# Turning two heads' out^T in one 128-row transpose, in an attention and feed-forward kernel

## Chip, cores and metric

The kernel runs on one core of a Trainium2 chip. The metric is the time of one execution on the device in microseconds; lower is better. Five engines work side by side, each through its own instructions in order: TensorE (PE in the profile; its weight loads PEld), VectorE (DVE), ScalarE (ACT), GpSimd (POOL) and SyncE (SP), whose queue issues the DMAs here.

## What is computed

Attention over 2 batches x 8 heads, 1152 keys of 64 dimensions, with neighbouring queries averaged in pairs (576 queries), then two gated feed-forward layers over the 1152 tokens. All is float32.

```python
q_pool = q.reshape(B, H, S // 2, 2, D).mean(axis=3)          # B, H, S, D = 2, 8, 1152, 64
scores = scale * np.matmul(q_pool, k.transpose(0, 1, 3, 2))
attn = np.exp(scores - scores.max(-1)); attn = attn / (attn.sum(-1) + 1e-09)
x = (attn @ v) -> (B * S // 2, H * D)                          # 1152 tokens of 512
xn = x / sqrt(mean(x * x) + 1e-06) * rms_g                     # layer 1
x = (silu(xn @ w_gate) * (xn @ w_val)) @ w_out                 # d_ff 1536
out = (sigmoid(x @ w_gate2) * (x @ w_val2)) @ w_out2           # layer 2
```

## The kernel before

**Tiles and chunks.** The 576 queries of a head are five chunks: chunks 1 to 4 hold 128 queries each, and chunk 0, the odd one, the last 64. Part 0 of a head is chunks 0 to 2 (320 queries), part 1 chunks 3 and 4 (256). Heads go in pairs (0 and 1, 2 and 3, ...); a pair's Q and K are loaded and turned together, the two heads side by side in 128 columns. Head 0 of a pair is called the even one here, head 1 the odd one.

**The stages of attention.** Scores (`s_unit`): PE multiplies Q by 384 keys at a time into a PSUM bank `s`, DVE (L543) copies the bank to `e` and takes the maximum, ACT exponentiates. For each head there are then 18 units, one for each key block of 128 and each part. A unit (`t_unit`) turns its two or three blocks of `e` by PE transposes into a bank `eT`; ACT, DVE or POOL copies the bank out, as high and low parts (`et`) or as one float32 (`ef`). Some slots later `av_unit` multiplies by V and adds up in a bank `o`: 128 columns for `et`, two products of 64 columns side by side for `ef`. A bank `o` has two halves of 64 partitions whose sum is out^T. After the last key block ACT copies one half to `osb` and DVE adds the other. The banks rotate: two for `s`, four for `eT` and all other transposes, two for `o`.

**Where the change works.** `o_step` turns out^T back: for each chunk of a part PE takes `osb` (64 partitions x 128 queries) as a transpose of 64 rows into the bank `oT`; ACT copies `oT` to `os` (L650), POOL multiplies by the reciprocal of the sums, `rcp`, into `x` (L648). So a head has two groups of oT, one of three and one of two transposes. In before the odd chunk is cut short elsewhere too: Q's sum of neighbours has a POOL instruction of its own for chunk 0 with 64 rows (L353), `q_transposes` turns chunk 0 with 64 rows through the helper `transpose` (L380), and so does `tr` in `x_steps` for the odd chunk of x, four transposes of 64 rows in each batch. `load_pair` fills only rows 0 to 63 of chunk 0 of Q.

**Order.** The order is written by hand: `at(g, rank, fn)` puts a step into slot g, and `run_agenda` writes the slots out in order, by rank within a slot. A head takes 18 slots. Every engine then goes through its own instructions in that order, and waits where a tile is not ready or a bank is still read. The scores of a pair are put 15 slots ahead of its use. At the end of attention the slots are filled with the first feed-forward products, while x of batch 1 is normed and turned. In the layers each weight block is loaded and split into two parts (L244 to L285) while earlier ones are in use.

Of the kernel before, what the change touches and what calls it, by code (L numbers as in the profile page):

```python
# [16 lines left out]
P = 128  # L17
# [78 lines left out]
def tile_attention_moe_moe(ctx, tc, q, k, v, w_gate1, w_val1, w_out1, rms_g, w_gate2, w_val2, w_out2, out):  # L96
# [234 lines left out]
    def load_pair(p):  # L331
        b, hp = divmod(p, NPAIR)
        kr = ap.tile([P, NK, P], F32, tag="kraw", bufs=1, name="kraw")
        qr = ap.tile([P, 2, NQC, 2 * D], F32, tag="qraw", bufs=1, name="qraw")
        qs = q[b, 2 * hp:2 * hp + 2].rearrange("j (s two) d -> j s (two d)", two=2)
        for j in range(2):
            nc.sync.dma_start(qr[:, j, 1:NQC, :], qs[j, 0:SQ - QH, :].rearrange("(c p) e -> p c e", p=P))
        nc.sync.dma_start(qr[0:QH, :, 0, :], qs[:, SQ - QH:SQ, :].rearrange("j p e -> p j e"))
        for j in range(2):

            nc.sync.dma_start(kr[:, :, j * D:(j + 1) * D], k[b, 2 * hp + j].rearrange("(p c) d -> p c d", c=NK))
        raw[p] = (kr, qr)
# [5 lines left out]
    def pool_q(p):  # L348
        kr, qr = raw[p]
        qs = ap.tile([P, NQC, P], F32, tag="qsum", bufs=1, name="qsum")  # L350
        qd = qs.rearrange("p c (j d) -> p j c d", j=2)
        nc.gpsimd.tensor_tensor(qd[:, :, 1:NQC], qr[:, :, 1:NQC, 0:D], qr[:, :, 1:NQC, D:2 * D], op=ALU.add)
        nc.gpsimd.tensor_tensor(qd[0:QH, :, 0], qr[0:QH, :, 0, 0:D], qr[0:QH, :, 0, D:2 * D], op=ALU.add)  # L353
        raw[p] = (kr, qs)

    def prep_v(i):
# [9 lines left out]
            nc.tensor.transpose(t[:, c * P:(c + 1) * P], raw[p][0][:, 4 * g + c, :], ident)  # L366
        return t[:, 0:n * P], slice(4 * g * P, (4 * g + n) * P)

    def q_transposes(p, g):
        t = bank("t", "qT")  # L370
        c0, c1 = ((0, 3), (3, NQC))[g]
        cs = slice(QCOL[c0], QCOL[c1] if c1 < NQC else SQ)
        for c in range(c0, c1):
            transpose(t, QCOL[c] - cs.start, raw[p][1][:, c, :], c)
        return t[:, 0:cs.stop - cs.start], cs

    def transpose(t, o, x, c, half=0):

        r = slice(0, P) if c else slice(half * QH, (half + 1) * QH)
        nc.tensor.transpose(t[:, o:o + r.stop - r.start], x[r], ident[r, r])  # L380
# [13 lines left out]
    def prep_first():  # L394
# [47 lines left out]
            return t[HP, 0:3 * P], slice(3 * g * P, 3 * (g + 1) * P)  # L442

        def head0(g0, is_k, g):
            t, cs = k_group(0, g) if is_k else q_transposes(0, g)
            if is_k:
                at(g0, 12, lambda: nc.scalar.activation(ka[HP, cs], t, AF.Copy))
                at(g0, 16, lambda: nc.vector.tensor_tensor(ka[LP, cs], t, ka[HP, cs].bitcast(F32), op=ALU.subtract))
            else:
                at(g0, 12, lambda: nc.scalar.activation(qa[:, 0, cs], t, AF.Copy, scale=QSC))  # L450
                at(g0, 16, lambda: nc.vector.scalar_tensor_tensor(qa[:, 1, cs], t, QSC, qa[:, 0, cs].bitcast(F32), op0=ALU.mult, op1=ALU.subtract))

        def head1(g0, is_k, g):
            t, cs = k_group(1, g) if is_k else q_transposes(0, g)
            hi, lo = (kb[HP, cs], kb[LP, cs]) if is_k else (qb[:, 0, cs], qb[:, 1, cs])
            sc = 1.0 if is_k else QSC
            at(g0, 13, lambda: nc.scalar.activation(hi, t, AF.Copy, scale=sc))
            if (is_k, g) in SECOND_DVE:
                at(g0 + 1, 19, lambda: nc.vector.scalar_tensor_tensor(lo, t, sc, hi.bitcast(F32), op0=ALU.mult, op1=ALU.subtract))
                return  # L460
            r = ae.tile([P, 512], F32, tag="kqt", bufs=3, name="kqt")[0:t.shape[0], 0:t.shape[1]]
            at(g0, 13, lambda: nc.scalar.activation(r, t, AF.Copy, scale=sc))
            at(g0 + 1, 21, lambda: nc.gpsimd.tensor_tensor(lo, r, hi.bitcast(F32), op=ALU.subtract))
# [44 lines left out]
    def s_unit(g, p, k):  # L508
# [40 lines left out]
                nc.gpsimd.tensor_copy(sums[i + 1][h * QH:(h + 1) * QH, 0:1], sums[i][(1 - h) * QH:(2 - h) * QH, 0:1])  # L549

        def recip():
            rcp[i] = ae.tile([P, NQC, 1], F32, tag="rc", bufs=2, name="rc")
            nc.vector.tensor_scalar_add(sums[i], sums[i], 1e-9)
            nc.vector.reciprocal(rcp[i][:, :, 0], sums[i])

        at(g, 17, top)
        if u == NSU - 1:
# [46 lines left out]
    def av_unit(g, i, j, et, parts):  # L604
        part, kc = part_of(i, j)
        n = NB if part else NA
        if kc == 0:
            oacc[i, part] = bank("o", "o")
        o = oacc[i, part]
        if parts:  # L610
            for k in range(2):
                nc.tensor.matmul(o[:, 0:n], vv[i][:, kc, :], et[:, k, 0:n], start=(kc == 0 and k == 0), stop=(kc == NK - 1 and k == 1))  # L612
        elif kc % 2 == 0:
            ets[i] = et
        else:

            for r, c, x in ((HP, kc - 1, ets[i]), (LP, kc, et)):
                nc.tensor.matmul(o[r, 0:n], vraw[i][:, c, :], x[:, 0:n], start=(kc == 1), stop=False)  # L618
        if kc == NK - 1:
            if i not in osb:  # L620
                osb[i] = ae.tile([D, SQ], F32, tag="osb", bufs=2, name="osb")
            ob = osb[i][:, part * NA:part * NA + n]
            at(g, 11, lambda: nc.scalar.activation(ob, o[HP, 0:n], AF.Copy))
            at(g, 18, lambda: nc.vector.tensor_tensor(ob, o[LP, 0:n], ob, op=ALU.add))
            g += 1 if i == NHEAD - 1 and part else 2
            at(g, 7, lambda: o_step(g, i, part))

    def o_step(g, i, part):

        b, h = divmod(i, H)  # L630
        if b not in xall:
            if b == B - 1:
                xa = ae.tile([P, NCA, DM], F32, tag="xa", bufs=1, name="xa")
                xb = ae.tile([P, NQC - NCA, DM], F32, tag="xb", bufs=1, name="xb")
            else:

                xa, xb = [xpool.tile([P, NDM * (NT - NX0) // DM, DM], F32, tag=f"x{s}1", name="x") for s in "hl"]
            xall[b] = ((xa, 0, NCA), (xb, NCA, NQC))
        x, c0, c1 = xall[b][part]
        n = c1 - c0  # L640
        t = bank("t", "oT")
        for c in range(c0, c1):
            nc.tensor.transpose(t[:, (c - c0) * D:(c - c0 + 1) * D], osb[i][:, QCOL[c]:QCOL[c] + P], ident[HP, HP])  # L643
        os = ae.tile([P, NCA, D], F32, tag="os", bufs=1, name="os")[:, 0:n]
        xs = x[:, 0:n, h * D:(h + 1) * D]

        def norm():
            nc.gpsimd.tensor_tensor(xs, os, rcp[i][:, c0:c1, :].to_broadcast([P, n, D]), op=ALU.mult)  # L648

        at(g + 1, 14, lambda: nc.scalar.activation(os.rearrange("p c d -> p (c d)"), t[:, 0:n * D], AF.Copy))  # L650
        at(g + 1, 41, norm)
        if h == H - 1:
            x_steps(g + 2, b, part)

    def x_steps(g, b, part):
# [28 lines left out]
        def tr(g, c):  # L684
            t = bank("o" if last else "t", "xT")
            for dc in range(NDM):
                transpose(t, dc * P, xp[:, c, dc * P:(dc + 1) * P], c0 + c)
            n = P if c0 + c else QH
            src = t.rearrange("p (c f) -> p c f", f=P)
            t0 = b * SQ + ((c0 + c - 1) * P if c0 + c else SQ - QH)  # L690
# [240 lines left out]
```

## Time and profile before

| | |
|---|---|
| median of three runs | 763.41 us (762.86 to 763.51) |
| the profiled execution | 763.09 us, span 761.3 us |
| PE busy | 751.4 us, 99% of the span |
| DVE, ACT, POOL busy | 464.8, 420.4, 391.1 us |
| opening, attention, hand-over, layers | about 0 to 31, to 292, to 320, to the end |
| oT transposes | 80, of 64 rows |

The profile names a line L..., an engine, an operation and the tiles written and read (out<-in). Matmuls on PE overlap: each is listed with its whole length, and the next one starts before it ends. What one costs is therefore seen in the starts of its neighbours. In a timeline consecutive instructions of one line and tile are merged, with their count (x3). A transpose is a matmul with the tile as its weights and an identity as the moving data, and the form 64*128 means 64 rows and 128 columns of the array; 128*64 is 128 rows and 64 columns.

### The profile page before, as it was taken

The page shows a single profiled execution, that of the slowest core. Times are in us where ns is not written, and L with a number is a line of the kernel's source. Part 1 is how long each engine was busy: PE and PEld are TensorE (multiplying, and loading weights), DVE is VectorE, ACT ScalarE, POOL GpSimd, SP SyncE. Part 2 cuts the span into 40 slices and gives each one's busy share as a digit, 9 for nine tenths or more (in the row PEclk, how much of TensorE's full clock was granted, in tenths as well). Part 3 has the DMA queues.
Part 4 walks back from the last instruction along what each step waited for, and adds up shares of the span by engine and source line. Part 5 has one row for each costly group of instructions (what it writes and reads, how often), then busy time and mean ns, then how long its engine had stood idle before and what let it go on. Part 6 is the DMA issues. An engine that isn't in the chain of part 4 may idle for free.

```text
span 761.3 us, 13230 instructions
## 1 busy us (share of the span) xinstructions
PE 751.4 (99%) x4865; PEld 696.0 (91%) x4865; DVE 464.8 (61%) x1150; ACT 420.4 (55%) x903; POOL 391.1 (51%) x456
## 2 busy tenths in 40 slices
PE   8999999999999999999899999999999999999998
PEld 6678888889888888999799999999999999999998
DVE  7777787878787887766666675442265546453000
ACT  6577777778887875454544444533354445445100
POOL 6567678678787771244443445743254345437100
PEclk9999999999999999999999999999999999999999
DMA  8535463827274210033322232431122222222101
GB/s 224 113 76 125 121 150 84 185 50 183 67 165 100 70 44 1 29 96 98 93 79 82 81 111 87 136 111 56 56 83 84 84 84 85 82 84 84 63 1 63
DMA packets 70400, 69.82 MB, mean 92 GB/s; under 512 B 19200, under 2 KB 61824, under 8 KB 70336
## 3 DMA queue, kind: packets, MB, share of 16 engines
q1 hardware_dynamic: 70336, 68.99, 33.1%
q8 instruction: 38, 0.62, 0.3%
q14 instruction: 26, 0.21, 0.1%
HBM read 52.17 MB, written 2.36 MB: 72 GB/s over the span
## 4 chain that ended last, share of the span: by engine, by line
PE 94%; DVE 2%; ACT 1%; issue 1%; POOL 1%; DMA 0%; ACTq 0%
PE acc L760 38%; PE s L539 11%; PE acc L878 10%; PE acc L855 10%; PE eT L380 9%; PE o L612 7%; PE o L618 4%; PE eT L579 2%; PE oT L643 1%; DVE e L543 1%; PE kT L366 1%; PE qT L380 1%; PE xT L380 1%; DMA first<-in_q_dram 0%; ACT wg L244 0%
## 5 line engine op out<-in xcount | busy, mean ns | idle before, releaser
L760 PE MATMUL acc<-xh,w 128*128 128x384 f32 (+2 forms) x1184 | 298.5, 333 | 3.1 <-DVE sg L773 3.0
L760 PEld LDWEIGHTS acc<-xh,w 128*128 128x128 f32 x1184 | 212.6, 188 | 4.7 <-DVE sg L773 4.6
L760 PE MATMUL acc<-xl,w 128*128 128x384 f32 (+2 forms) x592 | 196.4, 332 | 0.0
L285 POOL TENSOR_TENSOR w<-wr,w 128x512 fp32r<-128x512 f32 x72 | 101.8, 1414 | 154.4 <-ACT w L284 154.4
L543 DVE TENSOR_SCALAR_CACHE_REDUCE e<-s 128x384 f32<-128x384 f32 (+1 forms) x219 | 120.3, 554 | 46.7 <-PE s L539 43.3
L244 ACT ACTIVATE wg<-wraw 128x512 f32<-128x512 f32 x72 | 48.3, 670 | 150.4 <-issue 111.2
L272 POOL TENSOR_TENSOR wr<-wsg,wr 128x512 uint32<-128x512 uint32 x72 | 93.3, 1296 | 65.3 <-DVE wsg L271 62.2
L380 PE MATMUL eT<-ident,e 128*128 128x128 f32 (+1 forms) x594 | 113.8, 275 | 0.0
L539 PE MATMUL s<-kk,qq 128*128 128x384 f32 (+1 forms) x396 | 110.0, 362 | 1.4 <-DVE e L543 1.1
L760 PEld LDWEIGHTS acc<-xl,w 128*128 128x128 f32 x592 | 111.1, 188 | 0.0
L558 ACT ACTIVATE e<-e,nb 128x1152 f32<-128x1152 f32 (+1 forms) x73 | 91.4, 1252 | 0.3 <-DVE nb L545 0.3
L380 PEld LDWEIGHTS eT<-ident,e 128*128 128x128 f32 (+1 forms) x594 | 76.4, 140 | 16.3 <-issue 6.0
L612 PE MATMUL o<-et,vv 128*128 128x320 f32 (+1 forms) x380 | 90.4, 334 | 0.0
L774 DVE TENSOR_TENSOR sg<-acc,sg 128x384 f32<-128x384 f32 (+2 forms) x74 | 40.5, 547 | 75.4 <-PE acc L760 40.4
L878 PE MATMUL acc<-w,hh 128*128 128x256 f32 x432 | 76.7, 281 | 0.0
L599 ACT ACTIVATE et<-eT 128x320 fp32r<-128x320 f32 (+1 forms) x139 | 56.4, 414 | 34.5 <-PE eT L380 28.7
L539 PEld LDWEIGHTS s<-kk,qq 128*128 128x128 f32 (+1 forms) x396 | 61.2, 187 | 15.2 <-DVE e L543 4.8
L855 PE MATMUL acc<-hh,w 128*128 128x384 f32 x288 | 73.5, 335 | 0.0
L271 DVE SCALAR_TENSOR_TENSOR wsg<-wg,wsg 128x512 uint32<-128x512 uint32 x72 | 65.5, 910 | 2.3
L878 PEld LDWEIGHTS acc<-w,hh 128*128 128x128 f32 x432 | 66.5, 189 | 0.0
L781 DVE TENSOR_TENSOR hl<-sg,hh 128x384 fp32r<-128x384 f32 (+2 forms) x74 | 62.9, 851 | 4.0 <-ACT hh L780 4.0
L600 DVE TENSOR_TENSOR et<-eT,et 128x320 fp32r<-128x320 f32 (+1 forms) x139 | 63.3, 457 | 3.1 <-ACT et L599 2.4
(113 smaller groups left out, 1132.3 us busy)
## 6 DMA issues: line engine op xcount, KB each, us to landing
wraw<-in_moe_w_gate_dram SPq DMA_DIRECT2D x24, 512.0 KB, 3.6
wraw<-in_moe_w_val_dram SPq DMA_DIRECT2D x24, 512.0 KB, 3.6
wraw<-in_moe_w_out_dram SPq DMA_DIRECT2D x24, 512.0 KB, 3.7
qq<-qq SPq DMA_DIRECT2D x21, 288.0 KB, 3.2
vraw<-in_v_dram SPq DMA_DIRECT2D x16, 288.0 KB, 2.9
kraw<-in_k_dram SPq DMA_DIRECT2D x14, 288.0 KB, 5.5
kk<-kh SPq DMA_DIRECT2D x14, 288.0 KB, 4.1
kk<-kl SPq DMA_DIRECT2D x14, 288.0 KB, 4.7
```

Of the source, the lines that this page charges most:

```text
L271: nc.vector.scalar_tensor_tensor(sg, g, 3, sg, op0=ALU.logical_shift_left, op1=ALU.bitwise_or)
L272: nc.gpsimd.tensor_tensor(r, sg, r, op=ALU.add)
L285: nc.gpsimd.tensor_tensor(t[:, 1], r, t[:, 0].bitcast(F32), op=ALU.subtract)
L380: nc.tensor.transpose(t[:, o:o + r.stop - r.start], x[r], ident[r, r])
L539: nc.tensor.matmul(s[r, 0:SU], qs, ks[:, kc], start=(n1 == 0), stop=(n1 == len(products) - 1))
L543: nc.vector.tensor_scalar(e[r, kc], s[r, 0:SU], 1.0, None, op0=ALU.mult, op1=ALU.max, accum_out=m[r, u:u + 1])
L558: at(g + EXP_LAG, 12, lambda: nc.scalar.activation(e[r], e[r], AF.Exp, bias=nb[r], scale=1.0, accum_out=sums[i][r, c:c + 1]))
L600: at(g + 1, 20, lambda: nc.vector.tensor_tensor(et[:, 1, 0:n], t, et[:, 0, 0:n].bitcast(F32), op=ALU.subtract))
L612: nc.tensor.matmul(o[:, 0:n], vv[i][:, kc, :], et[:, k, 0:n], start=(kc == 0 and k == 0), stop=(kc == NK - 1 and k == 1))
L760: nc.tensor.matmul(acc[:, 0:nt], wt[:, ws, dc * P:(dc + 1) * P], xs[:, dc], start=(dc == 0 and n == 0), stop=(dc == NDM - 1 and n == 2))
L855: nc.tensor.matmul(acc[t][:, 0:NTT], w[:, ws, (fc % 4) * P:(fc % 4 + 1) * P], hs[fc][:, cs], start=(fc == 0 and n == 0), stop=(fc == NFC - ...
L878: nc.tensor.matmul(acc[r // 2][:, (r % 2) * HC:(r % 2 + 1) * HC], hs[fc][:, r * P:(r + 1) * P], w[:, ws, (fc % 2) * HC:(fc % 2 + 1) * HC], ...
```

## The change

Both heads of a pair put their out^T into one `osb` of 128 partitions: the even head into partitions 0 to 63, the odd one into 64 to 127 (ACT and DVE swap the halves of `o` for it). `o_step` is only called behind the odd head, and turns both heads at once, with 128 rows and the whole identity. The reciprocals of both heads lie in one tile `rcp` with two columns per chunk, `os` and POOL's product are twice as wide. For the odd chunk of Q rows 64 to 127 are filled with queries that nobody uses (one more DMA per pair, of the first 64 queries), POOL's sum is one instruction, and the transpose has 128 rows; its 64 superfluous columns are written over by the next chunk's transpose. Pair 0, whose Q is loaded in another way, keeps its 64 rows. The odd chunk of x is turned with 128 rows too.

```diff
@@ -335,7 +335,9 @@
         qs = q[b, 2 * hp:2 * hp + 2].rearrange("j (s two) d -> j s (two d)", two=2)
         for j in range(2):
             nc.sync.dma_start(qr[:, j, 1:NQC, :], qs[j, 0:SQ - QH, :].rearrange("(c p) e -> p c e", p=P))
-        nc.sync.dma_start(qr[0:QH, :, 0, :], qs[:, SQ - QH:SQ, :].rearrange("j p e -> p j e"))
+
+        for r, x in ((slice(0, QH), SQ - QH), (slice(QH, P), 0)):
+            nc.sync.dma_start(qr[r, :, 0, :], qs[:, x:x + QH, :].rearrange("j p e -> p j e"))
         for j in range(2):
             nc.sync.dma_start(kr[:, :, j * D:(j + 1) * D], k[b, 2 * hp + j].rearrange("(p c) d -> p c d", c=NK))
@@ -349,8 +351,7 @@
         kr, qr = raw[p]
         qs = ap.tile([P, NQC, P], F32, tag="qsum", bufs=1, name="qsum")
         qd = qs.rearrange("p c (j d) -> p j c d", j=2)
-        nc.gpsimd.tensor_tensor(qd[:, :, 1:NQC], qr[:, :, 1:NQC, 0:D], qr[:, :, 1:NQC, D:2 * D], op=ALU.add)
-        nc.gpsimd.tensor_tensor(qd[0:QH, :, 0], qr[0:QH, :, 0, 0:D], qr[0:QH, :, 0, D:2 * D], op=ALU.add)
+        nc.gpsimd.tensor_tensor(qd, qr[:, :, :, 0:D], qr[:, :, :, D:2 * D], op=ALU.add)
         raw[p] = (kr, qs)
     def prep_v(i):
@@ -366,12 +367,13 @@
             nc.tensor.transpose(t[:, c * P:(c + 1) * P], raw[p][0][:, 4 * g + c, :], ident)
         return t[:, 0:n * P], slice(4 * g * P, (4 * g + n) * P)
-    def q_transposes(p, g):
+    def q_transposes(p, g, whole=True):
         t = bank("t", "qT")
         c0, c1 = ((0, 3), (3, NQC))[g]
         cs = slice(QCOL[c0], QCOL[c1] if c1 < NQC else SQ)
         for c in range(c0, c1):
-            transpose(t, QCOL[c] - cs.start, raw[p][1][:, c, :], c)
+
+            transpose(t, QCOL[c] - cs.start, raw[p][1][:, c, :], c or whole)
         return t[:, 0:cs.stop - cs.start], cs
     def transpose(t, o, x, c, half=0):
@@ -442,7 +444,7 @@
             return t[HP, 0:3 * P], slice(3 * g * P, 3 * (g + 1) * P)
         def head0(g0, is_k, g):
-            t, cs = k_group(0, g) if is_k else q_transposes(0, g)
+            t, cs = k_group(0, g) if is_k else q_transposes(0, g, False)
             if is_k:
                 at(g0, 12, lambda: nc.scalar.activation(ka[HP, cs], t, AF.Copy))
                 at(g0, 16, lambda: nc.vector.tensor_tensor(ka[LP, cs], t, ka[HP, cs].bitcast(F32), op=ALU.subtract))
@@ -451,7 +453,7 @@
                 at(g0, 16, lambda: nc.vector.scalar_tensor_tensor(qa[:, 1, cs], t, QSC, qa[:, 0, cs].bitcast(F32), op0=ALU.mult, op1=ALU.subtract))
         def head1(g0, is_k, g):
-            t, cs = k_group(1, g) if is_k else q_transposes(0, g)
+            t, cs = k_group(1, g) if is_k else q_transposes(0, g, False)
             hi, lo = (kb[HP, cs], kb[LP, cs]) if is_k else (qb[:, 0, cs], qb[:, 1, cs])
             sc = 1.0 if is_k else QSC
             at(g0, 13, lambda: nc.scalar.activation(hi, t, AF.Copy, scale=sc))
@@ -549,9 +551,10 @@
                 nc.gpsimd.tensor_copy(sums[i + 1][h * QH:(h + 1) * QH, 0:1], sums[i][(1 - h) * QH:(2 - h) * QH, 0:1])
         def recip():
-            rcp[i] = ae.tile([P, NQC, 1], F32, tag="rc", bufs=2, name="rc")
+            if p not in rcp:
+                rcp[p] = ae.tile([P, NQC, 2], F32, tag="rc", bufs=2, name="rc")
             nc.vector.tensor_scalar_add(sums[i], sums[i], 1e-9)
-            nc.vector.reciprocal(rcp[i][:, :, 0], sums[i])
+            nc.vector.reciprocal(rcp[p][:, :, j], sums[i])
         at(g, 17, top)
         if u == NSU - 1:
@@ -617,17 +620,21 @@
             for r, c, x in ((HP, kc - 1, ets[i]), (LP, kc, et)):
                 nc.tensor.matmul(o[r, 0:n], vraw[i][:, c, :], x[:, 0:n], start=(kc == 1), stop=False)
         if kc == NK - 1:
-            if i not in osb:
-                osb[i] = ae.tile([D, SQ], F32, tag="osb", bufs=2, name="osb")
-            ob = osb[i][:, part * NA:part * NA + n]
-            at(g, 11, lambda: nc.scalar.activation(ob, o[HP, 0:n], AF.Copy))
-            at(g, 18, lambda: nc.vector.tensor_tensor(ob, o[LP, 0:n], ob, op=ALU.add))
+
+            p, odd = divmod(i, 2)
+            if p not in osb:
+                osb[p] = ae.tile([P, SQ], F32, tag="osb", bufs=2, name="osb")
+            r1, r2 = (LP, HP) if odd else (HP, LP)
+            ob = osb[p][r1, part * NA:part * NA + n]
+            at(g, 11, lambda: nc.scalar.activation(ob, o[r1, 0:n], AF.Copy))
+            at(g, 18, lambda: nc.vector.tensor_tensor(ob, o[r2, 0:n], ob, op=ALU.add))
             g += 1 if i == NHEAD - 1 and part else 2
-            at(g, 7, lambda: o_step(g, i, part))
-
-    def o_step(g, i, part):
-
-        b, h = divmod(i, H)
+            if odd:
+                at(g, 7, lambda: o_step(g, p, part))
+
+    def o_step(g, p, part):
+
+        b, hp = divmod(p, NPAIR)
         if b not in xall:
             if b == B - 1:
                 xa = ae.tile([P, NCA, DM], F32, tag="xa", bufs=1, name="xa")
@@ -640,16 +647,20 @@
         n = c1 - c0
         t = bank("t", "oT")
         for c in range(c0, c1):
-            nc.tensor.transpose(t[:, (c - c0) * D:(c - c0 + 1) * D], osb[i][:, QCOL[c]:QCOL[c] + P], ident[HP, HP])
-        os = ae.tile([P, NCA, D], F32, tag="os", bufs=1, name="os")[:, 0:n]
-        xs = x[:, 0:n, h * D:(h + 1) * D]
+            nc.tensor.transpose(t[:, (c - c0) * P:(c - c0 + 1) * P], osb[p][:, QCOL[c]:QCOL[c] + P], ident)
+        os = ae.tile([P, NCA, P], F32, tag="os", bufs=1, name="os")[:, 0:n]
+        xs = x[:, 0:n, hp * P:(hp + 1) * P]
         def norm():
-            nc.gpsimd.tensor_tensor(xs, os, rcp[i][:, c0:c1, :].to_broadcast([P, n, D]), op=ALU.mult)
-
-        at(g + 1, 14, lambda: nc.scalar.activation(os.rearrange("p c d -> p (c d)"), t[:, 0:n * D], AF.Copy))
+            def by_head(t):
+                return t.rearrange("p c (j d) -> p c j d", j=2)
+
+            r = rcp[p][:, c0:c1].rearrange("p c (j o) -> p c j o", o=1)
+            nc.gpsimd.tensor_tensor(by_head(xs), by_head(os), r.to_broadcast([P, n, 2, D]), op=ALU.mult)
+
+        at(g + 1, 14, lambda: nc.scalar.activation(os.rearrange("p c d -> p (c d)"), t[:, 0:n * P], AF.Copy))
         at(g + 1, 41, norm)
-        if h == H - 1:
+        if hp == NPAIR - 1:
             x_steps(g + 2, b, part)
     def x_steps(g, b, part):
@@ -684,7 +695,7 @@
         def tr(g, c):
             t = bank("o" if last else "t", "xT")
             for dc in range(NDM):
-                transpose(t, dc * P, xp[:, c, dc * P:(dc + 1) * P], c0 + c)
+                nc.tensor.transpose(t[:, dc * P:(dc + 1) * P], xp[:, c, dc * P:(dc + 1) * P], ident)
             n = P if c0 + c else QH
             src = t.rearrange("p (c f) -> p c f", f=P)
             t0 = b * SQ + ((c0 + c - 1) * P if c0 + c else SQ - QH)
```

Three places show what moves. The first is PE in the second half of an even head, between the products `s` and `o`; `eT` are the turned scores. Before:

```order
L380 MATMUL eT<-ident,e 128x128 x2
L612 MATMUL o<-et,vv 128x256 x2
L539 MATMUL s<-kk,qq 128x384 x2
L380 MATMUL eT<-ident,e 128x128 x2
L643 MATMUL oT<-ident,osb 128x64 x3
L539 MATMUL s<-kk,qq 128x384 x2
L380 MATMUL eT<-ident,e 128x128 x2
L612 MATMUL o<-et,vv 128x256 x4
```

The same place in the changed kernel, whose lines have other numbers:

```order
L541 MATMUL s<-kk,qq 128x384 x2
L382 MATMUL eT<-ident,e 128x128 x2
L541 MATMUL s<-kk,qq 128x384 x2
L382 MATMUL eT<-ident,e 128x128 x2
L615 MATMUL o<-et,vv 128x256 x4
```

The group of three oT is gone, and s follows eT. All other instructions of PE stand in the order of before.

The second is PE at the same point of the next, odd head. Before:

```order
L612 MATMUL o<-et,vv 128x256 x2
L539 MATMUL s<-kk,qq 128x384 x2
L380 MATMUL eT<-ident,e 128x128 x2
L643 MATMUL oT<-ident,osb 128x64 x3
L612 MATMUL o<-et,vv 128x256 x2
```

And changed:

```order
L615 MATMUL o<-et,vv 128x256 x2
L541 MATMUL s<-kk,qq 128x384 x2
L382 MATMUL eT<-ident,e 128x128 x2
L650 MATMUL oT<-ident,osb 128x128 x3
L615 MATMUL o<-et,vv 128x256 x2
```

The group stays where it was, with outputs of 128 columns in place of 64.

The third is POOL near the end of an odd head: `qsum` is the sum of neighbouring queries, `vv` and `qq` are splits into high and low parts, `x` is the product with the reciprocals. Before:

```order
L352 TENSOR_TENSOR qsum<-qraw 128x2x4x64
L353 TENSOR_TENSOR qsum<-qraw 64x128
L178 TENSOR_SCALAR vv<-vraw 128x9x64
L179 TENSOR_TENSOR vv<-vraw,vv 128x9x64
L648 TENSOR_TENSOR x<-os,rc 128x3x64
L549 COPY sums<-sums 64x1 x2
L178 TENSOR_SCALAR qq<-kqt 128x320
```

And changed:

```order
L354 TENSOR_TENSOR qsum<-qraw 128x2x5x64
L178 TENSOR_SCALAR vv<-vraw 128x9x64
L179 TENSOR_TENSOR vv<-vraw,vv 128x9x64
L659 TENSOR_TENSOR x<-os,rc 128x3x128
L551 COPY sums<-sums 64x1 x2
L178 TENSOR_SCALAR qq<-kqt 128x320
```

The sum of Q is one instruction, and the product is of double width at the same place. The two products of the even head are gone. ACT loses its two copies to `os` of the even head, DVE's order is unchanged, and SP has one more DMA for Q per pair from pair 1 on.

## Rows read from the trace of the kernel before

**Rows 1.** The profile's page: busy time, share, count of PE and others; the last chain by engine.

```profile
PE 751.4 (99%) x4865; PEld 696.0 (91%) x4865; DVE 464.8 (61%) x1150; ACT 420.4 (55%) x903; POOL 391.1 (51%) x456
...
PE 94%; DVE 2%; ACT 1%; issue 1%; POOL 1%; DMA 0%; ACTq 0%
```

**Rows 2.** Table of stretches: us, busy time (count) of each engine, granted clock, DMA share, GB/s.

```profile
31.00:292.00 261.00, 261.00 (x1805) 216.62 (x1803) 209.45 (x707) 205.13 (x477) 186.19 (x277) 1.00 0.46 108
...
320.00:760.00 440.00, 435.20 (x2698) 433.69 (x2696) 212.34 (x320) 182.16 (x353) 180.37 (x133) 1.00 0.26 83
```

**Rows 3.** Groups by shape: busy us, mean ns of one, idle before.

```profile
L643 PE MATMUL oT<-ident,osb 64*128 64x64 f32 x80 | 11.7, 242 | 0.0
...
L468 PE MATMUL warm<-ident 128*128 128x128 f32 x8 | 2.0, 427 | 1.3 <-POOL ident masks.py:199 1.3
```

**Rows 4.** Timeline of PE, 105 to 108 us: start, length, instruction, count (merged).

```profile
105.15 0.38 PE L380 MATMUL eT<-ident,e 128*128 128x128 f32 x2
105.46 0.40 PE L643 MATMUL oT<-ident,osb 64*128 64x64 f32 x3
105.78 0.62 PE L539 MATMUL s<-kk,qq 128*128 128x384 f32 x2
106.24 0.38 PE L380 MATMUL eT<-ident,e 128*128 128x128 f32 x2
...
106.94 0.38 PE L380 MATMUL eT<-ident,e 128*128 128x128 f32 x2
107.07 0.59 PE L539 MATMUL s<-kk,qq 128*128 128x384 f32 x2
107.51 0.38 PE L380 MATMUL eT<-ident,e 128*128 128x128 f32 x2
```

**Rows 5.** Timeline of PE, 96 to 98 us.

```profile
96.85 0.38 PE L380 MATMUL eT<-ident,e 128*128 128x128 f32 x2
97.16 0.34 PE L643 MATMUL oT<-ident,osb 64*128 64x64 f32 x2
...
97.88 0.27 PE L579 MATMUL eT<-swap_id,e 128*128 128x128 f32 x1
```

**Rows 6.** Timeline of PE, 100 us.

```profile
100.10 0.60 PE L366 MATMUL kT<-ident,kraw 128*128 128x128 f32 x4
100.45 0.54 PE L612 MATMUL o<-et,vv 128*128 128x320 f32 x2
```

**Rows 7.** Timeline of PE, 91 to 93 us.

```profile
91.36 0.38 PE L380 MATMUL eT<-ident,e 128*128 128x128 f32 x2
91.67 0.64 PE L380 MATMUL qT<-ident,qsum 64*128 64x64 f32 x3
92.24 0.65 PE L618 MATMUL o<-ef,vraw 128*64 128x256 f32 x4
```

**Rows 8.** The chain that ended last, 301 to 305 us: start, length, what.

```profile
301.81 1.28 ACT L771
...
303.55 0.47 DVE sg L773
...
304.07 1.88 PE acc L760 x12
```

**Rows 9.** Groups by shape, POOL's product of out with the reciprocal.

```profile
L648 POOL TENSOR_TENSOR x<-os,rc 128x192 f32<-128x192 f32 x8 | 4.1, 507 | 1.7 <-ACT os L650 1.6
```

**Rows 10.** DMA issues by line: count, KB each, median us to landing.

```profile
qraw<-in_q_dram SPq DMA_DIRECT2D x7, 64.0 KB, 4.4
```

**Rows 11.** Timeline of DVE and PE, two places.

```profile
104.86 0.56 DVE L543 TENSOR_SCALAR_CACHE_REDUCE e<-s 128x384 f32<-128x384 f32 x1
...
79.42 0.48 DVE L600 TENSOR_TENSOR et<-eT,et 128x320 fp32r<-128x320 f32 x1
...
80.31 0.27 PE L579 MATMUL eT<-ident,e 128*128 128x128 f32 x1
```

**Rows 12.** Timeline of PE, second part of the layers.

```profile
368.74 0.44 PE L760 MATMUL acc<-xh,w 128*128 128x384 f32 x1 [1.00 <-DVE sg L773]
```

## The prediction

> **What bounds the kernel now.** I read the page first, then the table of stretches, then the timeline of TensorE with the other engines beside it. The page has PE busy for 99% of the span and 94% of the last chain on PE [rows 1]. The table shows that this holds in the part that the change touches: from 31 to 292 us, attention, PE is busy in every microsecond, while DVE, ACT and POOL work in 71 to 80% of it [rows 2]. After a hand-over (292 to 320 us) come the two feed-forward layers, 440 us in which nothing is changed. So the question is what one PE instruction adds to PE's stream, and that is read from starts, not from the "busy" of one: a transpose of 64 rows is listed with 0.24 us [rows 3], which says nothing about what it makes its neighbours wait.
>
> **A group of 64-row transposes.** I take a stretch from one eT group to the next, with and without oT between. With three oT: eT at 105.15, the next eT at 106.24, 1.09 us. The same two eT and two s without oT: 106.94 to 107.51, 0.57 us [rows 4]. So the group of three costs 0.52 us. The group of two: 96.85 to 97.88, 1.03 us [rows 5], so 0.46 us. The third transpose is 0.06 us; about 0.34 us of every group is entry and exit: 0.2 us from the last 128-row eT to the first oT, 0.15 to the s behind, and 0.1 more inside that s pair. Where an o pair follows instead of s, starts nearby give the same to 0.01.
>
> **A group of 128-row transposes.** The trace has these already, as kT between eT and o: four start at 100.10, and the next product, o, at 100.45 [rows 6]. That is three steps of 0.11 and 0.03 to the product, which is what a product behind eT waits too (106.94, two eT, s at 107.07) [rows 4]. So a 128-row transpose among others adds 0.11 us and no entry or exit. Three cost 0.33, two 0.22.
>
> **Part 1: out^T.** Each of 8 pairs has four groups now (3 and 2 transposes per head). The change drops those of the even head and makes those of the odd head 128 rows high.
> - Even heads: 8 x (0.52 + 0.46) = 7.84 us. One group (head 6) stands before ef products of 64 columns, which wait 0.2 us behind any 128-row transpose; it saves 0.32, not 0.46. Sum 7.7.
> - Odd heads: 8 x (0.52 - 0.33) + 8 x (0.46 - 0.22) = 3.44. The last group, at 303.1 us, lies just ahead of a wait (below), so its 0.24 is not counted. Sum 3.2.
>
> **Part 2: Q's odd chunk.** One 64-row and two 128-row qT: last eT group at 91.36, qT at 91.67, products at 92.24 [rows 7]. All with 128 rows: five steps of 0.11 and the same 0.2 before the ef products give 92.00. That is 0.24 a time. Seven pairs have it; that of pair 1 lies in the opening, where PE then waits for others, and counts nothing. 6 x 0.24 = 1.45 us.
>
> **Part 3: x's odd chunk.** Two groups of four. The first stands between a 128-row eT and ef products: now 0.20 + 0.11 + 2 x 0.06 + 0.15, then 4 x 0.11 + 0.20, a loss of 0.05. The second lies in the hand-over and is hidden. Taken as 0.
>
> **The hand-over.** Behind the xT of that second group ACT loads its table at 301.81 (1.28 us) and does the sigmoid, DVE multiplies at 303.55, and this frees the bank that PE uses at 304.07 [rows 8]. What PE saves between 300.9 and 304 only makes it wait longer there; hence the two zeros above. The wider copies lie on the same way: POOL's product of 192 columns takes 0.51 us [rows 9], one of 384 at most twice that, so x's norm may start up to 0.5 us later in each of its two parts, and with ACT's wider os not over 1 us in all. PE's own products ahead of 300.9 cover the first part; I take 0, and the 1 us goes into the range.
>
> **What others get.** ACT and POOL have, per pair, two copies and two products of double width in place of four, and POOL's sum of Q is one instruction, not two: less work for both. Queued behind the wider product on POOL are the swap of sums, the split of qq and then an et of the next head, for which PE waits; they come up to 0.5 us later. POOL idles for 29% of attention [rows 2] and an et has some slots between its split and its use, so I take 0; without any lead it would be 8 x 0.5 = 4 us, about what rival B takes. Seven DMAs of 64 KB come on top, ahead of K's two loads on SP's queue. They are issued 16 of a head's 18 slots before POOL sums Q, some 15 us (16 heads in about 290 us); the present ones land in 4.4 us [rows 10]. Taken as 0, and without that cover at most 4.4 us once per pair. DVE has the same instructions in the same order.
>
> **What is late next.** DVE is not idle everywhere. Around 105 us it has no gap, and its L543 of 104.86 ends at 105.42 [rows 11]; this frees the bank of the s that starts at 105.78 [rows 4]. From DVE's end to PE's start it takes 0.05 us (304.02 to 304.07) [rows 8], so s can start at 105.47 at the earliest: 0.31 of the 0.52 arrives, 0.21 turns into a wait. This pattern comes back behind the group of three of an even head in six of eight pairs (in one of them with 0.14), 1.2 us. Beside it: behind the group of two of an even head, eT at 80.31 writes a bank whose last reader, L600, ends at 79.90 [rows 11]. Room 0.35 against 0.46, five times 0.1, if the ring of four banks still pairs these two; since oT takes a bank less often, it may be 0. I take 0.5 for this and a few single places of that kind.
>
> **Sum.** 7.7 + 3.2 + 1.45 = 12.35 us off PE's stream; 1.2 + 0.5 = 1.7 given back; 10.65 us net. The profiled execution took 763.09 us with a span of 761.3, the median is 763.41. 763.4 - 10.65 = **752.8 us** (1.4%).
>
> **Rivals.**
> - *A: nothing is given back.* DVE's stretches without a gap begin where it waits for PE's s, so DVE may move forward as PE does. Then 763.4 - 12.35 = 751.1. Against it: the s at 105.78 and its L543, which have no removed work between the start of the gapless stretch and themselves.
> - *B: DVE takes much more.* If half of the even heads' 7.7 us is turned into waits for DVE (it works 80% of attention, and the shorter stream raises this to 84%), the net is 10.65 - 3.85 = 6.8, or 756.6. For it: the gapless stretches. Against: between them DVE waits for PE in nearly every head.
> - *C: a 128-row transpose costs what it is listed with.* One alone is listed with 0.27 us (eT at 80.31) [rows 11], against steps of 0.11. With 40 oT and 6 qT that would be 46 x 0.16 = 7.4 us less gain, 760.2. Against: kT in rows 6. The Trainium skill, page "TensorE: Matmul & The Clock Gate", Part 4, gives about 275 ns for a 128x128 transpose in a kernel's context and so speaks for C; the trace agrees with it as the time of one, and not as the step.
> - *D, slower: the clock.* The granted clock is 1.00, the upper level of 2.4 GHz, over all of attention [rows 2]. In the opening eight transposes side by side took 2.0 us, the last of them 0.43 [rows 3]: 1.57 / 7 = 0.22 a step against 0.11, which I read as the lower level of 1.2 GHz. If the new waits, with more transposes side by side, let the clock fall, one pair of heads (35 us) would take up to twice as long: 752.8 + 35 = 788. It decides from 10.65 us of PE work at the lower level on. Against it: PE stops for 1.0 us at 368.74 [rows 12] and the stretch around stays at 1.00 [rows 2]. The Trainium skill, in the same Part 4, holds that transposes do not engage the fast level as products do; no stretch here shows that.
>
> **How the numbers follow.** Forecast 0.60, A 0.14, B 0.19, C 0.04, D 0.03. The range 751.0 to 757.0 holds the forecast, most of A and B, and leaves out C and D; its ends are the two bounds of what DVE gives back. About 0.2% (1.5 us) can be told from no change here. Faster by more than that in the forecast, A, B and C as reckoned; I leave 0.02 of those for within 0.2%, where DVE takes all of it, and 0.03 for D: faster 0.95, same 0.02, slower 0.03.
>
> **What would show it.** Right: oT x3 between two eT and s no longer adds 0.52 but 0.33, and no entry of 0.2 us before oT and qT; 4865 matmuls become 4825 (80 oT to 40, the rest as before); the stretch from the first oT to the xT at 300.9 is 10 to 12 us shorter, the feed-forward layers as long as before. DVE's idle time for PE s shrinks, and small waits of PE for L543 appear behind the places where even heads had three oT. Wrong: steps of over 0.15 between the new oT (C), a granted clock under 1.00 in attention (D), PE waits for DVE that add up to more than 4 us (B), or waits for POOL's et behind the wide product, which I have at nothing.

## The result and the profile after

The changed kernel takes 752.99 us (median of 4 runs, 752.49 to 753.22) against 763.29 (762.86 to 763.51) of the kernel before on the same chip: a ratio of 0.9865, 95% interval 0.9848 to 0.9882, so 10.3 us less. The forecast was 752.8. The profiled execution took 753.13 us with a span of 751.1.

From the profile's page: busy time of the engines, the last chain by engine, and the group of DVE's `e` copy with its idle time (before, this copy idled 43.3 us for PE's s).

```profile
PE 740.7 (99%) x4825; PEld 692.8 (92%) x4825; DVE 463.1 (62%) x1150; ACT 419.7 (56%) x887; POOL 388.5 (52%) x433
...
PE 87%; issue 5%; ACT 4%; DVE 3%; POOL 1%; DMA 0%; ACTq 0%; DVEq 0%
...
L545 DVE TENSOR_SCALAR_CACHE_REDUCE e<-s 128x384 f32<-128x384 f32 (+1 forms) x219 | 120.0, 553 | 37.3 <-PE s L541 33.9
```

The table of stretches, as [rows 2]; attention now ends 10 us earlier:

```profile
31.00:282.00 251.00, 250.95 (x1770) 213.13 (x1769) 208.26 (x709) 204.67 (x462) 183.37 (x255) 1.00 0.48 114
...
310.00:750.00 440.00, 435.03 (x2694) 433.83 (x2692) 211.76 (x318) 181.67 (x351) 180.13 (x133) 1.00 0.27 83
```

PE lost 40 matmuls (4865 to 4825), stayed busy in nearly every microsecond of attention, and kept its clock at 1.00. DVE, ACT and POOL did about the same work in less time, and DVE's `e` copy idles 9.4 us less for PE. Now the timeline of PE at the odd head's two groups (start, length, instruction, count), to be laid beside [rows 4, 5]:

```profile
85.18 0.38 PE L382 MATMUL eT<-ident,e 128*128 128x128 f32 x2
85.40 0.49 PE L650 MATMUL oT<-ident,osb 128*128 128x128 f32 x3
85.64 0.48 PE L615 MATMUL o<-et,vv 128*128 128x256 f32 x2
...
93.87 0.38 PE L382 MATMUL eT<-ident,e 128*128 128x128 f32 x2
94.09 0.38 PE L650 MATMUL oT<-ident,osb 128*128 128x128 f32 x2
94.23 0.60 PE L541 MATMUL s<-kk,qq 128*128 128x384 f32 x2
```

From the eT to the first oT is 0.22, two steps of 0.11, as between any two eT; the product stands 0.14 behind the first of two oT (0.11 and 0.03). Entry and exit are gone. At the place of the even head's group of three, the timelines of DVE and then of PE show the give-back:

```profile
67.70 0.49 DVE L630 TENSOR_TENSOR osb<-o,osb 64x320 f32<-64x320 f32 x1
68.22 0.56 DVE L545 TENSOR_SCALAR_CACHE_REDUCE e<-s 128x384 f32<-128x384 f32 x1
68.71 0.08 DVE L545 DVE_READ_ACCUMULATOR e<-s 128x1 f32 x1
```

```profile
68.50 0.38 PE L382 MATMUL eT<-ident,e 128*128 128x128 f32 x2
68.85 0.62 PE L541 MATMUL s<-kk,qq 128*128 128x384 f32 x2
69.31 0.27 PE L382 MATMUL eT<-ident,e 128*128 128x128 f32 x1
```

Two eT at 68.50 with no oT behind them, and yet s starts 0.35 later instead of 0.14: it waits for the bank that DVE's copy lets go at 68.79. DVE stands there without a gap, and the addition of the even head's two halves (L630) is part of that row.

To see where the time went, I took the start of every s product, and of the layers' products, in both traces and subtracted: the lead of the changed kernel over before.

| what lies between | step of the lead, us | times | forecast |
|---|---|---|---|
| even head, group of three | 0.32 to 0.33 at five; 0.41, less 0.11 at the next s, at one; 0.59 and 0.50 at the first and last | 8 | 0.31 at six (0.38 at one of them), 0.52 at two |
| even head, group of two | 0.44 to 0.45; 0.28 for head 6; the last does not stand alone | 7 | 0.46, less 0.1 at five; 0.32 for head 6 |
| odd head, group of three | 0.19 to 0.24 | 7 | 0.19 |
| odd head, group of two | 0.22 to 0.23 | 7 | 0.24 |
| Q | 0.24 to 0.28 | 6 | 0.24 |
| lead at 290.4, at 293.35 and in the span | 10.89, 10.72, 10.2 | | 10.65 |

### The profile page after: what moved, and what is told of

It is laid out like the page before. It is cut to its first block, busy times and chain, and to the rows that moved or that the text cites. A ratio compares the mean times of both kernels' runs of the same rounds, so it can differ in the third digit from the quotient of the medians.

```text
span 751.1 us, 13102 instructions
## 1 busy us (share of the span) xinstructions
PE 740.7 (99%) x4825; PEld 692.8 (92%) x4825; DVE 463.1 (62%) x1150; ACT 419.7 (56%) x887; POOL 388.5 (52%) x433
## 4 chain that ended last, share of the span: by engine, by line
PE 87%; issue 5%; ACT 4%; DVE 3%; POOL 1%; DMA 0%; ACTq 0%; DVEq 0%
PE acc L771 32%; PE s L541 11%; PE acc L889 10%; PE acc L866 10%; PE eT L382 9%; PE o L615 7%; PE o L621 4%; PE eT L582 2%; ACT wg L244 1%; ACT wr L252 1%; DVE e L545 1%; PE kT L367 1%; DVE sg L784 1%; ACT w L284 1%; ACT sg L782 1%
```

## The experiments

Experiments 1 to 8 each make one change to one of the two kernels; 9 and 10 put two together. Each ratio is to the kernel before, run beside it.

**1. Q and x alone.** The kernel before with parts 2 and 3:

```diff
-            transpose(t, QCOL[c] - cs.start, raw[p][1][:, c, :], c)
+            transpose(t, QCOL[c] - cs.start, raw[p][1][:, c, :], c or whole)
...
-                transpose(t, dc * P, xp[:, c, dc * P:(dc + 1) * P], c0 + c)
+                nc.tensor.transpose(t[:, dc * P:(dc + 1) * P], xp[:, c, dc * P:(dc + 1) * P], ident)
```

> The kernel before with the odd chunks of Q and x turned with 128 rows, and out^T as before. Theory (entry and exit of a 64-row transpose among 128-row ones is what costs): 0.24 us for each of six Q groups, nothing for x; 763.3 - 1.45 = 761.8 us. In the trace qT follows eT after 0.11 us and no longer after 0.20. Rival (a 128-row transpose costs what it is listed with, 0.27 us): about 763.3 or slower.

Measured 761.86 us against 763.40, ratio 0.9982 (0.9973 to 0.9990).

**2. out^T alone**, the changed kernel with the Q and x of before (the diff above turned round):

> The changed kernel with Q's and x's odd chunks turned with 64 rows as before; only out^T is turned for both heads at once. Theory: 7.7 + 3.2 us off PE's stream less 1.7 given back, 763.3 - 9.2 = 754.1 us; with the run on Q and x alone the two add up to the whole change. Rival (both parts share the waits for DVE): this one alone gains nearly as much as the whole, 753.0.

Measured 754.02, ratio 0.9880 (0.9866 to 0.9893). In both pairs of traces the lead grows at six places by 0.23 to 0.27 and nowhere else by more than 0.2 in attention after the opening: that is Q, 1.5 us in the stream. Of the times the one comparison shows 1.5 and the other 1.0. x gives nothing net.

**3. One place instead of two.** If entering and leaving the 64-row form is what costs, the groups of three and two of a head are cheaper as five in one place. The kernel before, in 14 heads:

```diff
-            at(g, 7, lambda: o_step(g, i, part))
+            if i % H == H - 1:
+                at(g, 7, lambda: o_step(g, i, part))
+            elif kc == NK - 1 and i in half_done:
+                at(g, 7, lambda: (o_step(g, i, 1 - part), o_step(g, i, part)))
+            half_done.add(i)
```

> The kernel before, all transposes of 64 rows as they were and as many, but in 14 of 16 heads the group of three stands right ahead of the group of two, so that there are 18 groups and not 32; os has two buffers for it. Theory (0.34 us of a group is entry and exit, a transpose more is 0.06): 14 x (0.52 - 3 x 0.06) = 4.7 us off PE's stream, less about 1.2 us where s then waits for DVE behind the even heads' place and up to 0.5 at the odd heads' place: 759.5 to 760.3 us. Rival (the cost lies in the transposes themselves, their number or their rows): 763.3.

Measured 763.49, ratio 1.0001 (0.9992 to 1.0010): the time did not move. PE's timeline has the group as the theory wants it, 0.31 to the first oT and 0.46 to the s behind the five:

```profile
96.00 0.38 PE L380 MATMUL eT<-ident,e 128*128 128x128 f32 x2
96.31 0.52 PE L649 MATMUL oT<-ident,osb 64*128 64x64 f32 x5
96.77 0.61 PE L539 MATMUL s<-kk,qq 128*128 128x384 f32 x2
```

For a pair the lead over before gains 0.30 at the even head's freed place (not 0.52, since s then waits 0.20 for DVE's copy) and 0.51 at the odd one's, and loses twice 0.19 for the longer groups: 0.43 net. Nearly as much came back in every pair with both places through new waits: s for DVE (0.08), an o product for POOL's `et` (0.09, and 0.05 more at the next product), and eT for a bank after two oT banks were taken at once (0.09 and 0.08). What was left went at single places: the lead, 0.97 us at 140 us, is 0.32 at 149 us, where the second group of oT starts 0.4 us late behind ACT, and the rest goes from 261 us on.

**4. The same in one bank,** so that only one bank and one copy of five chunks are used:

```diff
-                at(g, 7, lambda: (o_step(g, i, 1 - part), o_step(g, i, part)))
+                at(g, 7, lambda: o_step(g, i, (0, 1)))
...
-        os = ae.tile([P, NCA, D], F32, tag="os", bufs=2, name="os")[:, 0:n]
+        os = ae.tile([P, NQC, D], F32, tag="os", bufs=1, name="os")[:, 0:n]
```

> The kernel before, with the two groups of 64-row transposes of a head (three and two) done as one group of five, for 14 of 16 heads, but now into one bank and with one copy of five chunks by ScalarE, where the experiment with one place took two banks and two copies. Theory (entering and leaving the 64-row form costs some 0.33 us a group, and what the other experiment lost were its doubled banks and copies): 14 x 0.33 = 4.6 less, 1.2 given back at the score products that stand behind VectorE, so about 760.0 us against 763.4. Rival (the waits for VectorE and GpSimd that stood in that trace come from the longer stop of TensorE's other work, not from the banks): 0.09 + 0.08 a pair come back through the banks alone, some 1.2, so 762.2. Rival (nothing of a group is saved, its transposes alone cost): 763.4.

Measured 762.0, ratio 0.9985 (0.9976 to 0.9994), the 762.2 of the first rival. The waits of eT for banks are gone; the 0.20 for DVE stays, and so does that for POOL, 0.12 and 0.05 now. In PE's timeline s follows the first of two o by 0.61, where it takes 0.43 at the same place in before (this run, then before):

```profile
84.12 0.38 PE L380 MATMUL eT<-ident,e 128*128 128x128 f32 x2
84.25 0.77 PE L612 MATMUL o<-et,vv 128*128 128x320 f32 x2
84.86 0.34 PE L539 MATMUL s<-kh,qbd 128*128 128x384 f32 x1
```

```profile
84.99 0.60 PE L612 MATMUL o<-et,vv 128*128 128x320 f32 x2
85.42 0.34 PE L539 MATMUL s<-kh,qbd 128*128 128x384 f32 x1
```

So entry and exit are real costs on PE's stream, but taking them away from one place to put a longer stop in another leaves most of the gain in other queues.

**5. What one 64-row transpose alone costs.** The changed kernel still had 18 such eT: the odd chunk of the first pair's scores. Here they have 128 rows, and so have the scores themselves:

```diff
-                if p == 0:
-                    nc.gpsimd.memset(sums[h][QH:P, 0:1], 1.0)
...
-        r = slice(0, P if c or both else QH)
+        r = slice(0, P)
...
-                transpose(t, o + QCOL[c] - part * NA, e[:, ks], c, half)
+                transpose(t, o + QCOL[c] - part * NA, e[:, ks], c or i < 2, half)
```

> The changed kernel with the odd chunk of the scores of pair 0 in 128 rows too (its rows 64 to 127 are scores of queries that nobody uses), so that 18 eT of 64 rows become 128-row transposes in heads 0 and 1. Theory: each such eT has 0.09 us of entry and 0.09 of exit, 18 x 0.19 = 3.3 us: 753.0 - 3.3 = 749.7, or up to 0.5 more where DVE is late. Rival (this stretch, 24 to 55 us, is bound by DVE and ACT as the opening is): 753.0.

Measured 748.09 (747.60 to 748.63), ratio 0.9803 (0.9789 to 0.9816), 4.9 us below the changed kernel and more than expected. PE in the changed kernel (one transpose of 64 rows and two of 128, merged), and the same place in this one:

```profile
35.78 0.51 PE L541 MATMUL s<-kk,qq 128*128 128x384 f32 x2
36.23 0.64 PE L382 MATMUL eT<-ident,e 64*128 64x64 f32 x3
36.62 0.54 PE L615 MATMUL o<-et,vv 128*128 128x320 f32 x2
```

```profile
33.06 0.51 PE L539 MATMUL s<-kk,qq 128*128 128x384 f32 x2
33.41 0.49 PE L382 MATMUL eT<-ident,e 128*128 128x128 f32 x3
33.66 0.54 PE L613 MATMUL o<-et,vv 128*128 128x320 f32 x2
```

From s to the product behind the eT it takes 0.84 with the 64-row transpose and 0.60 without, 0.24 more for a single one. This step of 0.24 or 0.25 stands at 17 of the 18 places, from 24 to 46 us of the changed kernel, and 0.09 at the other: 4.2 us, of which 3.9 are left, since an s product then starts 0.25 late at 31.97 of this run. The edit also makes twelve s products whole that had 64 columns; at the six behind 23 us the lead moves by no more than 0.05. The other 1.0 came at once, where most of PE's wait for DVE at 22.74 fell away, which the forecast for this run had not looked at (changed kernel, then this one):

```profile
22.74 0.62 PE L541 MATMUL s<-kk,qq 128*128 128x384 f32 x2 [1.06 <-DVE e L545]
```

```profile
21.21 0.48 PE L613 MATMUL o<-et,vv 128*128 128x256 f32 x2
21.75 0.61 PE L539 MATMUL s<-kk,qq 128*128 128x384 f32 x2
```

What of the first pair's scores made DVE late there was not taken apart.

**6. What a 128-row transpose costs.** The changed kernel with each oT written twice:

```diff
         for c in range(c0, c1):
-            nc.tensor.transpose(t[:, (c - c0) * P:(c - c0 + 1) * P], osb[p][:, QCOL[c]:QCOL[c] + P], ident)
+            for _ in range(2):
+                nc.tensor.transpose(t[:, (c - c0) * P:(c - c0 + 1) * P], osb[p][:, QCOL[c]:QCOL[c] + P], ident)
```

> The changed kernel with each of the pairs' 128-row transposes of out^T done twice into the same columns: 8 pairs x 5 = 40 transposes more and nothing else. Forecast's price (a 128-row transpose costs its step of 0.109 us on TensorE's stream): 40 x 0.109 = 4.4, less some 0.3 at the end of the heads where TensorE waits anyhow: 757.0 us against 753.0, slightly less where the later TensorE removes a wait of its own. Rival (it costs its listed length of 0.27): 753.0 + 10.8 = 763.8. Rival (TensorE has that much time over at these places): 753.0.

Measured 757.28, ratio to before 0.9922 (0.9906 to 0.9939). 4.29 us more than the changed kernel, for 40 transposes, are 0.107 each, where the single one is listed with 0.27: the prediction's rival C falls. The changed kernel's lead over this run steps by 0.32 to 0.33 at a group of three and by 0.22 at one of two.

```profile
85.50 0.38 PE L382 MATMUL eT<-ident,e 128*128 128x128 f32 x2
85.71 0.82 PE L651 MATMUL oT<-ident,osb 128*128 128x128 f32 x6
86.29 0.48 PE L615 MATMUL o<-et,vv 128*128 128x256 f32 x2
```

**7. Where the give-back comes from.** Nobody waits any more for the even head's `osb` before the pair's transposes 17 us later, so its addition can leave DVE's row ahead of the waiting s. The changed kernel with it three slots later:

```diff
-            at(g, 18, lambda: nc.vector.tensor_tensor(ob, o[r2, 0:n], ob, op=ALU.add))
+            at(*((g, 18) if odd else (g + 3, 26)), lambda: nc.vector.tensor_tensor(ob, o[r2, 0:n], ob, op=ALU.add))
```

> The changed kernel with one thing moved: VectorE's addition of the two halves of an even head's output (which now has nobody waiting for it until the pair's transposes) stands three slots later and behind the slot's other VectorE work. The forecast's theory (the gain is given back because the score product stands behind VectorE's e copy with no slack at the six places where the even head's transposes were): the addition is the odd 0.25 us in VectorE's queue there, so six waits of 0.20 us go, 1.2 less what smaller waits take back: 752.0 us against 753.0. Rival (VectorE is full over the whole stretch and the addition costs the same wherever it stands): the waits move three slots on, 752.8 to 753.2. Rival (the order of queued work about those places, not the addition, sets the wait): no wait changes, 753.0.

Measured 756.32, ratio to before 0.9910 (0.9895 to 0.9924): 3.3 us slower than the changed kernel. The theory was half right. At the six places the lead over the changed kernel grew by 0.23 to 0.25, as expected; but 15 us behind five of them s starts 0.77 us late and the next product another 0.11, and two waits of about 0.45 stand at the ends (one of them s in the first pair, which shares its bank with o and waits for the addition itself). DVE and then PE at one of the five:

```profile
81.54 0.16 DVE L547 TENSOR_REDUCE nb<-m 128x1 f32<-128x3 f32 x1
81.61 1.24 DVE L271 SCALAR_TENSOR_TENSOR wsg<-wg,wsg 128x512 uint32<-128x512 uint32 x1
82.77 0.41 DVE L589 COPY ef<-eT 128x256 f32<-128x256 f32 x1
```

```profile
83.71 0.44 PE L541 MATMUL s<-kh,qbd 128*128 128x384 f32 x1 [0.61 <-DVE e L545]
```

and GpSimd beside it in this kernel, then DVE and GpSimd in the changed one:

```profile
81.43 0.87 POOL L179 TENSOR_TENSOR et<-er,et 128x320 fp32r<-128x320 f32 x1
```

```profile
81.17 0.68 DVE L271 SCALAR_TENSOR_TENSOR wsg<-wg,wsg 128x512 uint32<-128x512 uint32 x1
```

```profile
81.27 1.32 POOL L179 TENSOR_TENSOR et<-er,et 128x320 fp32r<-128x320 f32 x1
```

In the changed kernel DVE's weight product starts 0.10 ahead of POOL's, takes 0.68, and POOL's takes 1.32. In this one DVE starts 0.18 behind POOL: POOL's takes 0.87 and DVE's 1.24. Whichever is second ends about as if it had begun after the first (81.85 + 0.87 is 82.72 against 82.59; 82.30 + 0.68 is 82.98 against 82.85). The Trainium skill, page "SBUF — State Buffer", section "Who interferes with whom", states that a VectorE instruction with two inputs in SBUF and a GpSimd instruction that reads SBUF exclude each other, and that the order of issue decides who blocks. The trace agrees. Five such DVE instructions lie in attention; all five took 1.24 here and 0.68 in the changed kernel. It was the addition of the *second* half, at 79.27 here, that put DVE late.

**8. Only the six additions that stand before the six waits** are late now:

```diff
+            late = not (odd or part) and 0 < p < 7
+            at(*((g + 3, 26) if late else (g, 18)), lambda: nc.vector.tensor_tensor(ob, o[r2, 0:n], ob, op=ALU.add))
```

> The changed kernel with VectorE's addition three slots later at the six waits alone: the first half's addition of the even heads 2 to 12, where the first late version moved every even head's two. In that version's trace the six waits of 0.20 us were gone, and new ones of 0.77 + 0.11 us stood some 15 us behind them, where the second half's addition had put VectorE's weight-unpacking product (two operands in SBUF) 0.18 us behind the start of a GpSimd product with two operands in SBUF: it took 1.24 us where it takes 0.68 otherwise. Theory: with the second halves' additions back in their place that product takes 0.68 again and no new wait stands, the six waits stay away: 753.0 - 1.15 = 751.9 us. Rival (VectorE is full, and late work of 0.5 us comes to light wherever it is put): new waits behind the added work, 753.0 or more.

Measured 751.63 (750.88 to 751.64, 5 runs), ratio to before 0.9844 (0.9831 to 0.9858); 1.4 us under the changed kernel, whose runs lie apart from these (752.49 at the lowest), though the intervals of the two ratios overlap and the kernel before was 0.3 us faster beside this run (763.03 against 763.29); in the traces the lead over the changed kernel is 1.5 us at the end of attention, in steps of 0.23 to 0.25 at the six places. PE at the place shown above, with s 0.14 behind eT:

```profile
68.42 0.38 PE L382 MATMUL eT<-ident,e 128*128 128x128 f32 x2
68.56 0.59 PE L541 MATMUL s<-kk,qq 128*128 128x384 f32 x2
```

and the five weight products in attention (min, median and max in ns):

```profile
L271 DVE SCALAR_TENSOR_TENSOR wsg<-wg,wsg x5: 681/681/683, 80.8 to 246.2; 128x512 uint32<-128x512 uint32 x5
```

All six waits are gone and no new one stands. This shows the cause of the 1.2 us given back: the addition's 0.5 us in DVE's row ahead of the s copy.

**9 and 10. Both together.** Experiment 5 with the late additions of 7, and then with those of 8:

> The changed kernel with the first pair's odd chunk of the scores in 128 rows as well (measured alone: 748.1 us) and the even head's addition three slots later. Theory (the two gains lie at different places of the stretch of the heads, the first pair before 47 us, the six waits from 68 us on): 748.1 - 1.0 = 747.1 us. Rival (the lead that the first pair gives is taken back where VectorE or GpSimd is late, so that gains don't add): 748.1.

Measured 752.07, ratio 0.9855 (0.9840 to 0.9869): slower than 5 alone by 4.0, with the same waits of 0.77 in its trace.

> The same six additions late, in the changed kernel with the first pair's odd chunk of the scores in 128 rows (748.1 us alone). Theory (the two gains lie in different places): 748.1 - 1.15 = 746.9 us. Rival (the six waits come back at another place of VectorE's queue once the pair before is ahead): 748.1.

Measured 746.69 (746.54 to 747.35), ratio to before 0.9784 (0.9771 to 0.9798), the fastest of all. It is 1.4 us under 5 alone, with 1.3 us of lead behind the six places in the trace: the gains of 5 and 8 add up.

## Why the prediction was right

- **Price of a 64-row group:** right. It was read from starts; experiment 6 confirms the 0.11 of a 128-row transpose, experiment 5 the price of entry and exit on another tile: 0.35 for one transpose, 0.24 more than a whole one, beside 0.46 for two and 0.52 for three. The Trainium skill, page "TensorEngine Tiling (Array Packing)", section "Key Properties", states that a change of tiling mode drains TensorE. The runs here show what a change costs, and not what TensorE does in that time. Two details of the working are off and leave its sums as they are. By the starts, the 0.34 of entry and exit is 0.18 ahead of the first oT (0.20 in place of 0.03), 0.05 behind it, 0.09 on the way to s and 0.02 inside the s pair, where the prediction has 0.1; and the 92.00 for Q is four steps of 0.11 and 0.20, not five.
- **Even and odd heads, Q:** right to 0.05 at each place, mostly to 0.02, as the table shows, but for the first group of three (0.59 for 0.52) and the five groups of two that were to wait for a bank (below).
- **x:** right. The first group loses the reckoned 0.05: from the last eT to the o products it takes 0.59 before (eT at 294.08) and 0.64 changed (eT at 283.31). The second group gains 0.16 in experiment 1, and the wait at the hand-over takes back 0.19. The first group, before and then changed:

```profile
294.28 0.46 PE L380 MATMUL xT<-ident,x 64*128 64x64 f32 x4
294.67 0.65 PE L618 MATMUL o<-ef,vraw 128*64 128x256 f32 x4
```

```profile
282.92 0.66 PE L382 MATMUL eT<-ident,e 128*128 128x128 f32 x4
283.42 0.60 PE L698 MATMUL xT<-ident,x 128*128 128x128 f32 x4
283.94 0.65 PE L621 MATMUL o<-ef,vraw 128*64 128x256 f32 x4
```

- **The give-back behind DVE:** right in place, size and number (six waits, five of 0.20, one of 0.14 with 0.11 behind it), and experiment 8 shows what they hang on.
- **The 0.5 of lesser places:** right in sum only. The bank waits behind the group of two were to be five of 0.1; none is there, 0.44 to 0.45 of the 0.46 arrived. In their place stand three single waits that the forecast had not named: s for DVE at 253.09 (0.10), xT for POOL at 267.09 (0.20), oT for DVE's addition into `osb` at 281.64 (0.18), 0.48 together. So the size was luck. The wait at 267.09 belongs to the part on out^T: it stands in experiment 2 too (268.70), and not in experiment 1. POOL's wider product of out and reciprocal heads the row without a gap that ends with the x that xT waits for; it is 0.21 longer, and PE is ahead besides. For POOL's `et`, where the prediction had a delay at nothing, no new wait of PE stands in attention. The wider product, before and then changed:

```profile
272.09 0.41 POOL L648 TENSOR_TENSOR xb<-os,rc 128x128 f32<-128x128 f32 x1 [3.12 <-ACT os L650]
```

```profile
262.31 0.62 POOL L659 TENSOR_TENSOR xb<-os,rc 128x256 f32<-128x256 f32 x1 [3.22 <-ACT os L661]
```

- **The hand-over:** right. PE's wait there rose and took back 0.17 of the lead (10.89 to 10.72).

```profile
293.35 0.40 PE L771 MATMUL acc<-xh,w 128*128 128x288 f32 x1 [0.44 <-DVE sg L784]
```

- **The layers "as before":** off by 0.5 in these two traces, but not through the change. The lead falls from 10.72 at 293 us by 0.35 up to 350 us, comes back by 358 us, where PE waits for DVE, and falls again by 0.48 to 10.24, where it stays. In that last stretch 120 matmuls that are the same in both kernels (from 383.23 us before, from 372.58 us changed) take 20.80 us before and 21.20 us changed, some 3 ns more each. They take 21.20 in experiment 3 too, all of whose oT have 64 rows, and 20.80 in experiments 5 and 9, which contain the whole change. What makes the difference stays open. So the sum was nearly exact at the hand-over (10.72 against 10.65), and the 10.3 between the medians is below it by about as much.
- **Rivals:** A falls, since the waits came; B, since the new ones of PE for DVE in attention add up to 1.6 us, not 4; C by experiment 6; D, since the granted clock is 1.00 throughout, with 40 more transposes side by side too. The profile gives 1.00 for the opening as well, so that the opening's step of 0.22 is the lower level, as D reads it, is not shown.

## What to carry over

Read what an instruction costs TensorE from the starts of its neighbours, with it and without it, and look for what switches the array's form: a single half-height transpose among whole ones cost three times as much as a whole one. Before counting such a saving, look for the bank that the next product needs and at the queue of the engine that frees it; then ask which work in that queue has lost its hurry through the change itself. When moving that work, watch whom it pushes: 0.43 us of VectorE work, moved, became 0.88 us of waiting because it changed which of two engines came first.

## What was not expected of the hardware

- The order in which VectorE and GpSimd start two products with both operands in SBUF decides who pays, and what TensorE pays: 0.68 and 1.32 us in one order, without a wait of TensorE; 1.24 and 0.87 in the other, and 0.88 us of TensorE's time at each of five places.
- A wait of TensorE ahead of an s product of 384 columns costs 0.10 to 0.11 us beyond itself where s otherwise follows another product: the step to the next one is then 0.28 in place of 0.18 (in experiment 7, 83.71 to 83.99). Behind transposes little is added, since the step is 0.26 there without a wait (before, 107.07 to 107.33).
